# State loaded as it lies and transposed by products with the identity, and a first batch in written order: one core of a Trainium2 chip

## The chip, the cores and the metric

The kernel runs on one core of one Trainium2 chip. The core has a matrix engine (PE in the profile, with its weight loads as PEld), a vector engine (DVE), a scalar engine (ACT), GpSimd (POOL) and SyncE (SP), which here only issues transfers. PE writes to PSUM, eight banks of 2 KB in each of 128 partitions; the other engines copy from there to SBUF, where matmul operands have to lie. The metric is the device time of one launch in microseconds (us); lower is better.

## The reference

Eight batches of an attention between 512 positions `x` and 32 state vectors `state`, in both directions, with 8 heads of 64 numbers; then a feed-forward layer with the activation g = h * tanh(softplus(h)), called Mish, over all 8 x 544 rows.

```python
scores = scale * x @ state.T;   a  = softmax(scores)     # B, H, 512, 32
xread  = a @ state
scores2 = scale * state @ x.T;  a2 = softmax(scores2)    # B, H, 32, 512
sread  = a2 @ x
rows   = concat([xread, sread], axis=2)                  # B, H, 544, 64
x      = rows.transpose(0, 2, 1, 3).reshape(B * 544, 512)
h      = x @ w_in                                        # 512 -> 2048
out    = mish(h) @ w_out                                 # 2048 -> 512
```

The two weights come as 8-byte floats, 8 MB each; the kernel makes 4-byte numbers of them from their two words.

## The kernel before

*Arithmetic.* xread is never formed. Since xread @ w_in = a @ (state @ w_in), the kernel multiplies the state with a slice of w_in (`sw_slice`) and the softmax with that (`gemm1`). The large products run in a 4-byte type that PE takes in one pass, and each operand is split in a high part (a rounded copy) and a low part (the difference), with three products in place of one: high x high, high x low, low x high. So behind most results stand a cast on ACT or DVE (`swh`, `ah`, `gh`, the high half of `wo`) and a subtraction on DVE (`swl`, `al`, `gl`, the low half).

*Slots.* A batch is worked off in eight slots j of 256 hidden columns. In each slot `gemm1` runs 12 matmuls into two PSUM banks `ph`; ACT takes Mish of them into `g`; DVE splits `g` into `gh` and `gl`; `gemm2` runs 24 matmuls (four blocks of tokens, six each) into four banks `acc`, which collect over the eight slots. `second` runs such a `gemm2`, whole or in halves, up to two slots behind its `gemm1` (LAG = 2). The two remaining banks, `misc` (tag "m"), serve everything else in turn: transposes, scores, `sw_slice` and state reads.

*Attention.* `state_blocks` makes `bd`, the transposed state with its heads on two halves of the partitions, so that heads can be multiplied two and four at a time in small tiles of 64 x 32. `x_transposed` (`xt`), `scores`, `soft1_e`, `soft1_n`, `soft1_a` make the softmax over the state, in its two parts `ah` and `al`. The other direction, called the state part here, is `soft2_m` and `soft2_e` (maximum, exp), `e2_transposed` and `sread` (two reads and `sreadT`). Batches 0 and 1 transpose x on PE; from batch 2 on x comes by strided transfers (`xq`, 32 per batch) and DVE transposes it. The attention of the next batch runs in pieces between the slots of this one.

*Batch 0* also makes the weights. Each 512 KB piece of w_in or w_out is loaded as words; ACT scales the high words (`scale_high`) and rounds the low words (`round_low`; POOL may do that), DVE joins them (`join_words`). Slot j + 1 needs piece j + 1 of w_in, and the accumulation of slot j needs piece j of w_out, split in two by `high_w_out` and `low_w_out`. The words, exp and Mish use two different tables of ACT, so a slot of batch 0 loads a table twice.

*Order.* The program is written out in Python; a scheduler with a model of the times then orders the instructions of each engine, by their place in the source and by when it takes them to be ready. `behind(...)` asks that what it encloses be issued after the instructions remembered in `last`; it is used by hand all through batch 0. All loads go through SP's queue in one order, except the state of batch 0, which ACT's queue issues. Buffers order loads too: pieces 4 to 7 of w_in wait for the join of an earlier piece, and piece 7 of w_out for the last use of batch 0's x, which lies in its place (`tag="wo7"`). `fill` issues products of no use to keep PE busy in the head.

The state of a batch is loaded in three transfers of 32 KB, for even heads, odd heads and even heads again, and two transposes make `bd` of it:

```python
sn = pool.tile([P, 3, D], F32, tag="sn", name=f"sn_{b}")
for i in range(3):
    (nc.sync if b else nc.scalar).dma_start(
        sn[:, i, :], state[b].rearrange("(c a) n d -> a c n d", a=2)[i % 2])
...
for s in range(2):
    nc.tensor.transpose(
        pt[:, s * P:(s + 1) * P], sn[:, s:s + 2].rearrange("p a d -> p (a d)"), ident)
```

Of the kernel before, what the change touches and what calls it, by code (L numbers as in the profile page):

```python
# [16 lines left out]
P = 128  # L17
# [10 lines left out]
FILL = 20, 2, 2, 4  # L28
# [9 lines left out]

@with_exitstack
def state_attention_mish_kernel(ctx, tc, x, state, w_in, w_out, out):  # L40

    nc = tc.nc
    nc.scalar.preload_act_table_set("exp_and_others")
# [54 lines left out]
    def scale_high(raw):  # L98

        y = raw[..., 1].bitcast(F32)  # L100
        last["words"] = nc.scalar.activation(y, y, AF.Prelu, scale=2.0 ** -112, alpha=-2.0 ** 32)  # L101

    def round_low(raw, by_pool=False):
        lw = raw[..., 0]
        if by_pool:
            nc.gpsimd.tensor_scalar(lw, lw, 0.876 * 2.0 ** -29, 0.49, ALU.mult, ALU.add)
        else:
            last["words"] = nc.scalar.activation(lw, lw, AF.Copy, scale=0.876 * 2.0 ** -29, bias=0.49)
# [8 lines left out]
    def join_words(raw, to):  # L117
        lw, hw = raw[..., 0], raw[..., 1]
        last["join"] = nc.vector.scalar_tensor_tensor(
            to.bitcast(U32), hw, 3, lw, ALU.logical_shift_left, ALU.bitwise_or)  # L120
# [31 lines left out]
    def high_w_out(j, w):  # L152
        wo[j] = const.tile([P, 2, 2, DM], F32R, tag=f"wo{j}", name=f"wo_{j}")
        last["woh"] = nc.vector.tensor_copy(wo[j][:, :, 1], w)

    def low_w_out(j, w):
        last["wo"] = nc.vector.tensor_sub(wo[j][:, :, 0], w, as_f32(wo[j][:, :, 1]))

    def load_state(b):

        sn = pool.tile([P, 3, D], F32, tag="sn", name=f"sn_{b}")
        for i in range(3):
            (nc.sync if b else nc.scalar).dma_start(
                sn[:, i, :], state[b].rearrange("(c a) n d -> a c n d", a=2)[i % 2])
        return sn

    def state_blocks(b, sn):
# [3 lines left out]
        for s in range(2):  # L171
            nc.tensor.transpose(
                pt[:, s * P:(s + 1) * P], sn[:, s:s + 2].rearrange("p a d -> p (a d)"), ident)
        nc.vector.tensor_copy(bd.rearrange("p s n -> p (s n)"), pt[:, :2 * P])
# [3 lines left out]
    fills = []  # L178
# [10 lines left out]
    xs0 = load_x(0)  # L189
# [3 lines left out]
    for _ in range(WARM):  # L193
        nc.tensor.matmul(warm[:, :P], ident, ident, start=True, stop=True)


    def attention(b, xs, sn, xq=None):
# [4 lines left out]
        def x_transposed(c):  # L202

            if xq is not None:
                xTs[c] = temp(f"xT_{b}_{c}")
                nc.vector.transpose(  # L206
# [4 lines left out]
            for i in range(NT):  # L211
                nc.tensor.transpose(  # L212
                    pt[:, i * P:(i + 1) * P], xs[:, c, i // 2, (i % 2) * P:(i % 2 + 1) * P], ident)
            xTs[c] = temp(f"xT_{b}_{c}")
            if b == 0 and c % 2:
                nc.vector.tensor_copy(xTs[c], pt)
            else:
                nc.scalar.copy(xTs[c], pt)

        def scores():  # L220

            pss = [misc(f"sc_{b}_{u}") for u in range(2)]
            for c in range(NC):
                o = slice(c * NS, (c + 1) * NS)
                for kc in range(2):
                    kp = slice(kc * 2 * P, (kc + 1) * 2 * P)
                    for u in range(2):
                        last["PE"] = nc.tensor.matmul(  # L228
                            pss[u][o, kp], bds[b][half(u), kc ^ u, o], xTs[c][half(u), kp],
# [5 lines left out]
            for u in range(2):  # L235
                o = scs.rearrange("n k (v u p) -> n k v u p", v=2, u=2)[:, :, :, u]
                i = pss[u].rearrange("n (k v p) -> n k v p", k=2, v=2)
                if b == 0 and u:
                    nc.vector.tensor_scalar_mul(o, i, 0.125)
                else:  # L240
                    last[b, "scs"] = nc.scalar.mul(o, i, 0.125)  # L241

        def fill(n, pt):

            for _ in range(n):
                last["PE"] = nc.tensor.matmul(  # L246
# [6 lines left out]
        def soft2_m(kc):  # L253
            nm = nms[kc] = pool.tile([P, 1], F32, tag="nm", name=f"nm_{b}_{kc}")
            nc.vector.tensor_reduce(nm, sc[kc], AX.X, ALU.max, negate=True)

        def soft2_e(kc):
            e2 = temp(f"e2_{b}_{kc}")
            sm = pool.tile([P, 1], F32, tag="sm", name=f"sm_{b}_{kc}")
            last[b, "exp2"] = nc.scalar.activation(e2, sc[kc], AF.Exp, bias=nms[kc], accum_out=sm)  # L260
            nc.vector.tensor_scalar_add(sm, sm, 1e-9)  # L261
            rs2[kc] = pool.tile([P, 1], F32, tag="rs", name=f"rs_{b}_{kc}")
            nc.vector.reciprocal(rs2[kc], sm)
# [6 lines left out]
        def e2_transposed(kc):  # L270
            e2 = e2s[kc]
            pt = misc(f"e2p_{b}_{kc}")
            for t in range(NT):
                nc.tensor.transpose(pt[:, t * P:(t + 1) * P], e2[:, t * P:(t + 1) * P], ident)  # L274
            e2T[kc] = temp(f"e2T_{b}_{kc}", (P, NT, P))
            nc.scalar.copy(e2T[kc].rearrange("p t n -> p (t n)"), pt)
# [14 lines left out]
        def transposed(pt, src):  # L291
            for t in range(NT):
                last["PE"] = nc.tensor.transpose(pt[:, t * P:(t + 1) * P], src[:, t * P:(t + 1) * P], ident)

        def soft1_e():
# [6 lines left out]
            for kc in two:  # L302
                if b == 0:
                    transposed(src[kc], sc[kc])
                else:
                    nc.vector.transpose(e1[kc], sc[kc])  # L306
            for kc in two:
                mx = small["mx"][kc]
                with behind(*(((0, "sub"),) if b == 0 and kc else ())):
                    nc.vector.tensor_reduce(mx, groups(src[kc]), AX.X, ALU.max)  # L310
                last[b, "sub"] = nc.vector.tensor_sub(groups(e1[kc]), groups(src[kc]), wide(mx))
                with behind(*(("words",) if b == 0 else ())):
                    last[b, "exp"] = nc.scalar.activation(e1[kc], e1[kc], AF.Exp)

        def soft1_n():
            for kc in two:
                sm, r1 = small["s1"][kc], small["r1"][kc]
                nc.vector.tensor_reduce(sm, groups(e1[kc]), AX.X, ALU.add)
                nc.vector.tensor_scalar_add(sm, sm, 1e-9)
                nc.vector.reciprocal(r1, sm)  # L320
                last[b, "e1"] = nc.vector.tensor_mul(groups(e1[kc]), groups(e1[kc]), wide(r1))

        def soft1_a():
            for kc in two:
# [3 lines left out]
                else:  # L328
                    at = temp(f"at_{b}_{kc}")
                    nc.vector.transpose(at, e1[kc])  # L330
                hi = pool.tile([P, S], F32R, tag=f"ah{kc}", name=f"ah_{b}_{kc}")
                lo = pool.tile([P, S], F32R, tag=f"al{kc}", name=f"al_{b}_{kc}")
                last[b, "ah"] = nc.scalar.copy(hi, at)
                last[b, "DVE"] = nc.vector.tensor_sub(lo, at, as_f32(hi))
# [7 lines left out]
        def sread(kc):  # L342
            pr = misc(f"srp_{b}_{kc}")
            for t in range(NT):
                for h4 in range(4):
                    o = slice(h4 * NS, (h4 + 1) * NS)
                    last["PE"] = nc.tensor.matmul(  # L347
                        pr[o, :D],
                        e2T[kc][:, t, o],
                        xs[:, h4, kc, t * D:(t + 1) * D],  # L350
# [4 lines left out]
            nc.vector.tensor_scalar_mul(srd[0][:, kc], pr[:, :D], rs2[kc])  # L355

        def sreadT():
            pt = misc(f"srTp_{b}")[:, :P]
            nc.tensor.transpose(pt, srd[0].rearrange("p k d -> p (k d)"), ident)
            ptv = pt.rearrange("p (c n) -> p c n", c=NC)  # L360
            hi, lo = (t[..., b * NS:(b + 1) * NS] for t in srT)
            nc.scalar.copy(hi, ptv)
            nc.vector.tensor_sub(lo, ptv, as_f32(hi))

        xt, s_, s1, s2, e2t, sr = x_transposed, scores, soft1, soft2, e2_transposed, sread
        if b == 0:
# [313 lines left out]
```

## Time and profile before

| | |
|---|---|
| median of 3 runs | 699.71 us (697.62 to 700.04) |
| profiled execution | 697.67 us, its span 695.9 us |
| granted PE clock over the span | 0.992 of full |
| instructions | 10040, of these 4142 matmuls |
| loads and stores | 41.81 MB, 60 GB/s over the span |
| HBM read, written | 32.24 MB, 8.91 MB |

Times in the profile are microseconds from the start of the span. A row of the timeline has the start, the duration, the engine, the source line, the operation, output<-inputs, shape and count, and in brackets the idle time of the engine before it with what ended it. A row of a stretch of time has the busy time and, in parentheses, the instructions of each engine. A row of groups has the count, the total, the mean in ns, and the idle time before. A matmul is shown busy until its modelled end, so that matmuls that follow each other closely overlap.

### The profile page before, as it was taken

Reading aid. Unit: us, or ns where it says so; the run is one execution under the profiler, and the core shown is the slowest. Engines: PE = TensorE matmul, PEld = TensorE weight load, DVE = VectorE, ACT = ScalarE, POOL = GpSimd, SP = SyncE. Lnnn points to the kernel's source line nnn. Section 1 sums busy time; section 2 is a strip of 40 time slices with the busy share of each in tenths; the row PEclk is TensorE's granted clock in tenths of the full one; section 3 lists DMA queues with packets and bytes.
Section 4 is the critical chain, followed back from the end, with each engine's and each line's share of the span. In section 5 each row is a group of like instructions: output and inputs, shape, how many; then the busy total and the mean of one; then the engine's idle time right before and its main releaser. Section 6 shows DMA issues by size and latency. Waiting matters only on the chain.

```text
span 695.9 us, 10040 instructions
## 1 busy us (share of the span) xinstructions
PE 680.2 (98%) x4142; PEld 516.8 (74%) x4142; DVE 344.9 (50%) x520; ACT 262.0 (38%) x415; POOL 12.6 (2%) x13
## 2 busy tenths in 40 slices
PE   6988999999999999999999999999999999999997
PEld 5866776577777777777777777777777788977785
DVE  1996697483349423753367333942384234332221
ACT  2896864261235212641146123531255113222110
POOL 0230000000000000000000000000000000000000
PEclk7999999999999999999999999999999999999999
DMA  9975223401023011311032102301000001000001
GB/s 316 360 248 182 34 34 101 78 10 57 10 73 50 1 61 37 74 18 61 7 86 37 58 4 71 48 6 61 30 31 1 1 1 61 0 9 23 0 1 60
DMA packets 75789, 41.81 MB, mean 60 GB/s; under 512 B 57056, under 2 KB 65248, under 8 KB 75744
## 3 DMA queue, kind: packets, MB, share of 16 engines
q1 hardware_dynamic: 75348, 41.08, 20.3%
q8 instruction: 32, 0.52, 0.3%
q10 hardware_dynamic: 396, 0.10, 0.1%
q14 instruction: 13, 0.11, 0.0%
HBM read 32.24 MB, written 8.91 MB: 59 GB/s over the span
## 4 chain that ended last, share of the span: by engine, by line
PE 93%; ACT 4%; DMA 1%; issue 1%; ACTq 0%; DVE 0%
PE acc L480 51%; PE ph L435 24%; PE swp L398 5%; PE ph_s L458 3%; PE acc_s L480 3%; PE sc L228 2%; PE srp L347 1%; DMA sn<-in_state_dram 1%; PE e2p L274 1%; PE acc L246 1%; ACT L409 1%; ACT wor L101 1%; ACT g L409 1%; PE xTp L212 0%; ACT L101 0%
## 5 line engine op out<-in xcount | busy, mean ns | idle before, releaser
L480 PE MATMUL acc<-wo,gh 128*128 128x512 f32 x1024 | 326.5, 400 | 0.0
L480 PEld LDWEIGHTS acc<-wo,gh 128*128 128x128 f32 x1024 | 188.5, 188 | 67.9 <-issue 22.5
L480 PE MATMUL acc<-wo,gl 128*128 128x512 f32 x512 | 201.2, 396 | 0.0
L409 ACT ACTIVATE g<-ph 128x512 f32<-128x512 f32 x128 | 74.2, 598 | 223.0 <-DVE gl L416 154.7
L414 DVE CAST gh<-g 128x1024 fp32r<-128x1024 f32 x64 | 44.2, 691 | 163.5 <-PE acc L480 146.2
L480 PEld LDWEIGHTS acc<-wo,gl 128*128 128x128 f32 x512 | 96.3, 188 | 23.2 <-DVE gl L416 0.8
L435 PE MATMUL ph<-ah,swh 128*128 128x512 f32 x256 | 84.2, 401 | 2.8 <-ACT swh L403 2.8
L416 DVE TENSOR_TENSOR gl<-g,gh 128x1024 fp32r<-128x1024 f32 x64 | 78.8, 1231 | 4.8
L435 PE MATMUL ph<-al,swh 128*128 128x512 f32 x256 | 79.9, 392 | 0.0
L435 PE MATMUL ph<-ah,swl 128*128 128x512 f32 x256 | 79.3, 393 | 0.0
L404 DVE TENSOR_TENSOR swl<-swp,swh 128x512 fp32r<-128x512 f32 (+1 forms) x72 | 42.8, 625 | 54.2 <-ACT swh L403 53.8
L435 PEld LDWEIGHTS ph<-ah,swh 128*128 128x128 f32 x256 | 47.4, 188 | 17.9 <-ACT swh L403 4.6
L435 PEld LDWEIGHTS ph<-al,swh 128*128 128x128 f32 x256 | 48.2, 188 | 10.2
L435 PEld LDWEIGHTS ph<-ah,swl 128*128 128x128 f32 x256 | 47.6, 188 | 10.6
L403 ACT CAST swh<-swp 128x512 fp32r<-128x512 f32 (+1 forms) x72 | 35.7, 547 | 22.5 <-PE swp L398 22.5
L398 PE MATMUL swp<-w_in_sb,bd 64*32 64x512 f32 (+1 forms) x576 | 41.6, 554 | 1.9 <-DVE sm L261 1.8
L409 ACT ACT_TABLE_LOAD x20 | 25.7, 1283 | 30.1 <-PE e2p L274 14.1
L489 ACT COPY o<-acc 128x512 f32<-128x512 f32 x16 | 9.4, 587 | 43.6 <-PE acc L480 27.4
L455 DVE TENSOR_TENSOR wl<-w_in_sb,wh 128x512 fp32r<-128x512 f32 x16 | 11.1, 692 | 29.1 <-PE ph_s L458 25.1
L206 DVE STREAM_TRANSPOSE xT<-xq 128x512 f32<-128x512 f32 x24 | 24.4, 1091 | 0.1
L487 DVE COPY o<-acc 128x512 f32<-128x512 f32 x16 | 11.0, 689 | 20.5 <-DMA out_dram<-o 14.5
L306 DVE STREAM_TRANSPOSE e<-scs 128x512 f32<-128x512 f32 x14 | 9.1, 691 | 24.1 <-ACT scs L241 24.1
(82 smaller groups left out, 529.5 us busy)
## 6 DMA issues: line engine op xcount, KB each, us to landing
x<-in_x_dram SPq DMA_DIRECT2D x32, 256.0 KB
wir<-in_moe_w_in_dram SPq DMA_DIRECT2D x16, 512.0 KB
wor<-in_moe_w_out_dram SPq DMA_DIRECT2D x16, 512.0 KB
out_dram<-o SPq DMA_DIRECT2D x32, 256.0 KB
xq<-in_x_dram SPq DMA_DIRECT2D x192, 32.0 KB
sn<-in_state_dram SPq DMA_DIRECT2D x21, 32.0 KB
out_dram<-o_s SPq DMA_DIRECT2D x8, 64.0 KB
sn<-in_state_dram ACTq DMA_DIRECT2D x3, 32.0 KB
```

The source lines that it names most:

```text
L206: nc.vector.transpose(xTs[c].rearrange("p (k v i g) -> p g k v i", k=2, v=2, g=4), xq[:, c].rearrange("p k (g v) d -> p g k v d", v=2))
L228: last["PE"] = nc.tensor.matmul(pss[u][o, kp], bds[b][half(u), kc ^ u, o], xTs[c][half(u), kp], start=True, stop=True)
L398: last["PE"] = nc.tensor.matmul(pw[kc][o, :], bds[b][half(kc), 0, o], w_in_sb[half(kc), c, f], start=True, stop=True)
L403: last["swh"] = nc.scalar.copy(hi[:, kc], pw[kc])
L404: last["swl"] = nc.vector.tensor_sub(lo[:, kc], pw[kc], as_f32(hi[:, kc]))
L409: last["mish"] = nc.scalar.activation(g[:, k * 512:(k + 1) * 512], ph, AF.Mish)
L414: nc.vector.tensor_copy(gh, g)
L416: last["gl"] = nc.vector.tensor_sub(gl, g, as_f32(gh))
L435: last["PE"] = nc.tensor.matmul(ph, l, r, start=(i == 0), stop=(i == len(seq) - 1))
L455: nc.vector.tensor_sub(lo, w, as_f32(hi))
L458: nc.tensor.matmul(ph[r][:, k * 256:(k + 1) * 256], l[:, c], srT[i][:, c], start=(c == 0 and n == 0), stop=(c == NC - 1 and n == 2))
L480: last["PE"] = nc.tensor.matmul(accs[key][t], g[:, sl], wo[fc // 2][:, fc % 2, w, :], start=(fc == 0 and n == 0), stop=(fc == NFC - 1 and ...
```

## The change

- `load_state` makes two transfers in place of three, each of four whole heads as they lie in memory. `state_blocks` multiplies each with the identity, twice, for the upper and the lower half of the partitions: four products in place of two transposes. The copy to `bd` orders the heads by a stride, and `scores` and `sw_slice` index it accordingly.
- A class `InOrder` wraps PE, DVE and ACT. While its switch is on, in batch 0, each instruction of an engine is issued after the one written before it. Batch 0 is written out as a sequence of its own, with one accumulation of lag; `behind` is left for loads.
- In batch 0 the parts of the next attention have fixed places: its state block and two x transposes end slot 4, the other two stand in slot 5 with the scores, `soft1_e` stands in slot 6, `soft1_n` and `soft1_a` in slot 7. Its state part (`soft2_m` to `sreadT`) goes to batch 1.
- POOL rounds low words of w_out only from slot 3 on; ACT does those of pieces 1 and 2. w_out's piece 7 is scaled in slot 6 and joined in slot 7.
- `soft1_n` interleaves its two halves in the order written; `gemm1` in slots 0 and 1 goes through both banks in turn; the last `fill` has 6 products in place of 4.
- The loads of `xq` and state for batch 2 stand behind all of batch 0, and x of batch 2 in slot 3 of batch 1.

```diff
-FILL = 20, 2, 2, 4
+FILL = 20, 2, 2, 6
...
+class InOrder:
+    on = False
+    def __init__(self, tc, engine):
+        self.tc, self.engine, self.last = tc, engine, None
+    def __getattr__(self, name):
+        method = getattr(self.engine, name)
+        def issue(*args, **kwargs):
+            with ExitStack() as st:
+                if InOrder.on and self.last is not None:
+                    st.enter_context(self.tc.issue_after(self.last))
+                made = method(*args, **kwargs)
+            self.last = getattr(made, "ins", made)
+            return made
+        return issue
...
+    pe, dve, act = (InOrder(tc, e) for e in (nc.tensor, nc.vector, nc.scalar))
...
-        sn = pool.tile([P, 3, D], F32, tag="sn", name=f"sn_{b}")
-        for i in range(3):
+        sn = pool.tile([P, 2, D], F32, tag="sn", name=f"sn_{b}")
+        for g in range(2):
             (nc.sync if b else nc.scalar).dma_start(
-                sn[:, i, :], state[b].rearrange("(c a) n d -> a c n d", a=2)[i % 2])
+                sn[:, g, :], state[b, 4 * g:4 * g + 4].rearrange("h n d -> (h n) d"))
...
-        for s in range(2):
-            nc.tensor.transpose(
-                pt[:, s * P:(s + 1) * P], sn[:, s:s + 2].rearrange("p a d -> p (a d)"), ident)
-        nc.vector.tensor_copy(bd.rearrange("p s n -> p (s n)"), pt[:, :2 * P])
+        for g in range(2):
+            for r in range(2):
+                pe.matmul(pt[half(r), g * P:(g + 1) * P], sn[:, g], ident, start=True, stop=True)
+        dve.tensor_copy(
+            bd.rearrange("p s (c n) -> p c s n", n=NS),
+            pt[:, :2 * P].rearrange("p (c s n) -> p c s n", s=2, n=NS))
...
+            for step, kc in ((total, 0), (guard, 0), (total, 1), (turn, 0), (guard, 1), (norm, 0), (turn, 1), (norm, 1)):
+                step(kc)
...
+        steps = [(k, i) for k in range(2) for i in range(6)]
+        if b == 0 and j < 2:
+            steps.sort(key=lambda s: s[1] // 2)
...
+    def product(b, j):
+        phs = gemm1(b, j, aTs[b], sw)
+        def finish():
+            g = mish(b, j, phs)
+            gh, gl = high_g(f"{b}_{j}", g)
+            pending.append((b, (2 * j, 2 * j + 1), (gh, gl), NT))
+            return lambda: low_g(g, gh, gl)
+        return finish
...
+    InOrder.on = True
...
+    finish = product(0, 1)
+    at1, _, read = attention(1, sn1)
+    for j in range(1, SLOTS):
+        if j < 7:
+            words(j + 1, j, j > 2)
+        if j == 6:
+            words(None, 7, True)
+        if j + 1 < SLOTS:
+            join_i(j + 1)
+        if j == 3:
+            for kc in range(2):
+                at0["m2"](kc)
+            for kc in range(2):
+                at0["e2"](kc)
+        if j == 4:
+            for kc in range(2):
+                at0["e2t"](kc)
+        if j == 5:
+            at0["srT"]()
+            at1["xt"](2)
+            at1["xt"](3)
+        if j == 6:
+            at1["s1e"]()
+        if j < 7:
+            join_o(j)
+        second((0, 1), True)
+        low = finish()
+        if j + 1 < SLOTS:
+            sw.update(sw_slice(0, j + 1, 1))
+        else:
+            sw.update(sw_slice(1, 0))
+        second((2, 3))
+        if j == 4:
+            for kc in range(2):
+                at0["sr"](kc)
+        if j == 7:
+            at1["s1n"]()
+            at1["s1a"]()
+            join_o(j)
+        low_o(j)
+        low()
+        if j == 4:
+            state_blocks(1, sn1)
+            at1["xt"](0)
+            at1["xt"](1)
+        if j == 5:
+            at1["s"]()
+        if j + 1 < SLOTS:
+            finish = product(0, j + 1)
+    InOrder.on = False
...
+    todo = [lambda: [at1[p](kc) for p in ("m2", "e2") for kc in range(2)]] + read
+    xqs = {2: new_xq(2)}
+    with behind("load"):
+        load_xq(2, xqs[2], range(4 * H))
+        sn_next = load_state(2)
...
+        if key == 1 and j < 2:
+            second((2 * j, 2 * j + 1), j == 0)
+        elif len(pending) > LAG:
             second()
```

More of the change, by code (lines that the diff above doesn't have):

```diff
@@ L387, in attention @@
         ]
-        return [], pieces, aT
+        return own, ahead, read
     def sw_slice(b, j, n=2):
@@ L511, in state_attention_mish_kernel, with second, words @@
     with behind("load"):
-        xs_next, sn_next = load_x(1), load_state(1)
+        xss[1], sn1 = load_x(1), load_state(1)
     load(("o", 4), ("o", 6), ("o", 5), ("i", 6), ("i", 7), ("o", 7))
-    first[0]()
-    with behind((0, "scs")):
-        scale_words(raws[0])
-    first[1]()
+    pending = []
+    def second(ts=None, keep=False):
+        k_, fcs, g_, nt = pending[0] if keep else pending.pop(0)
+        gemm2(k_, list(fcs), g_[0], g_[1], nt, ts)
+    def words(i=None, o=None, by_pool=False):
+        for raw, p in ((raws.get(i), False), (rawo.get(o), by_pool)):
+            if raw is not None:
+                round_low(raw, True) if p else None
+                scale_high(raw)
+                None if p else round_low(raw)
@@ L519, in state_attention_mish_kernel, with fill @@
+    def fill(i):
+        at0["fill"](FILL[i], accs[0][NT - 1])
+    sw, aTs = {}, {}
+    InOrder.on = True
+    at0, _, _ = attention(0, sn0)
+    aTs[0] = at0["aT"]
+    at0["xt"](0)
+    at0["xt"](1)
+    state_blocks(0, sn0)
+    at0["xt"](2)
+    at0["xt"](3)
+    at0["s"]()
+    words(0)
+    at0["s1e"]()
     new_accs(0, NT)
-    def fill(i):
-        with behind("PE"):
-            fills[0](FILL[i], accs[0][NT - 1])
     fill(0)
-    first[2]()
-    with behind((0, "exp")):
-        scale_words(raws[1])
@@ L529, in state_attention_mish_kernel @@
-    with behind((0, "e1")):
-        join_w_in(0, raws.pop(0))
-    with behind("PE", "words", "join"):
-        first[3]()
+    words(1)
+    at0["s1n"]()
+    join_i(0)
+    at0["s1a"]()
     fill(1)
-    with behind("PE", (0, "ah"), (0, "DVE")):
-        sw_next = sw_slice(0, 0, 1)
+    sw.update(sw_slice(0, 0, 1))
     fill(2)
-    ws = {}
-    with behind("swl"):
-        join_w_in(1, raws.pop(1))
-    with behind("swh", "join"):
-        scale_words(rawo[0])
-        ws[0] = join_w_out(0, rawo.pop(0))
@@ L638, in state_attention_mish_kernel @@
-        for _ in range((0, 0, 1, 1)[j] if key == 0 and j < 4 else 1 + (key == 0)):
+        if key + 1 < B and j == 0:
+            own, ahead, rd = attention(key + 1, sn_next, xqs.pop(key + 1))
+            aTs[key + 1] = own["aT"]
+            todo = todo + ahead + rd
+        g = split_g(f"{key}_{j}", mish(key, j, gemm1(key, j, aTs[key], sw)))
+        pending.append((key, (2 * j, 2 * j + 1), g, NT))
+        nb, nj = (key, j + 1) if j + 1 < SLOTS else (key + 1, 0)
+        if nb < B and nj % 2 == 0:
+            sw.update(sw_slice(nb, nj))
```

275 lines of the change are left out of this document (106 added, 169 removed).

## The prediction

> **What bounds the kernel now.** I read the page's busy shares first, then the view by stretches of time, because a share of 98% is a mean over stages with different limits.
>
> ```profile
> span 695.9 us, 10040 instructions
> ...
> PE 680.2 (98%) x4142; PEld 516.8 (74%) x4142; DVE 344.9 (50%) x520; ACT 262.0 (38%) x415; POOL 12.6 (2%) x13
> ```
> ```profile
> 25.80:118.80 93.00, 87.35 (x633) 64.64 (x632) 74.68 (x107) 70.45 (x97) 10.77 (x6) 1.00 0.45 141
> 118.80:140.00 21.20, 21.20 (x128) 12.62 (x126) 11.02 (x17) 5.68 (x11) 0.00 (x0) 1.00 0.44 94
> ```
>
> The columns are PE, PEld, DVE, ACT and POOL busy, then clock and DMA. Up to 118.8 us, where the second batch's first product ends, PE is idle for 93.00 - 87.35 = 5.65 us, and DVE and ACT are busy for three quarters of the time. After that PE has no idle time, so any matmul added there costs its full length and DVE, ACT and DMA are hidden. The change can win only in the first 119 us, and can lose anywhere. PE also wastes time while busy. Small products of 64x32 run side by side, so half a set takes as long as a whole one:
>
> ```profile
> 122.00:123.40 1.40, 1.06 (x8) 0.15 (x8) 1.00 1.03 310
> 125.00:126.40 1.40, 1.06 (x8) 0.15 (x8) 1.00 0.32 49
> ...
> 135.20:136.40 1.20, 1.04 (x2) 0.14 (x2) 1.00 0.35 54
> 139.10:140.40 1.30, 1.08 (x14) 0.17 (x14) 1.00 0.32 49
> 157.80:159.10 1.30, 1.09 (x16) 0.18 (x16) 1.00 0.00 0
> ```
> ```profile
> 129.00:130.40 1.40, 1.09 (x16) 0.47 (x16) 1.00 0.36 57
> 132.50:133.90 1.40, 1.09 (x16) 0.47 (x16) 1.00 0.30 47
> 204.90:206.50 1.60, 1.13 (x32) 0.61 (x32) 1.00 0.30 47
> ```
>
> These are the state-times-w_in product (first fence) and the scores (second). Batch 1 splits three sets, 1.0 us lost each. So what the change can touch, beside the head, is 5.65 + 3.0 = 8.65 us.
>
> The head shows in PE's timeline and in its clock (third number from the right in the stretches):
>
> ```profile
> 7.28 0.30 PE L172 MATMUL st<-ident,sn 128*128 128x128 f32 x1 [1.07 <-DMA sn<-in_state_dram]
> 9.88 0.47 PE L172 MATMUL st<-ident,sn 128*128 128x128 f32 x1 [2.29 <-DMA sn<-in_state_dram]
> 10.15 1.91 PE L212 MATMUL xTp<-ident,x 128*128 128x128 f32 x8
> 11.99 2.81 PE L228 MATMUL sc<-xT,bd 64*32 64x256 f32 x32
> 15.56 1.97 PE L293 MATMUL scT<-ident,scs 128*128 128x128 f32 x8 [0.76 <-ACT scs L241]
> ```
> ```profile
> 5.90:9.00 3.10, 0.61 (x4) 1.00 1.00 338
> 9.00:10.00 1.00, 0.12 (x1) 0.64 0.99 384
> 10.00:15.00 5.00, 4.80 (x41) 0.50 1.04 404
> 15.00:19.00 4.00, 3.44 (x16) 0.50 1.05 398
> ```
>
> The first state transpose needs two of the three loads and starts at 7.28; the second needs the third and starts at 9.88. In the stretch to 9 PE is busy for 0.61 of 3.10 us, and then the clock is at half until 19. Scores take 2.81 us there, 1.13 at full clock.
>
> **The change part by part.** The sum is made against the profiled execution's own 697.67 us, 2.0 below the median of 699.71.
>
> *State as it lies.* Two loads instead of three, so both have landed at 7.28, where the first transpose started. A 128-column matmul takes about 0.107 us at full clock (eight in 1.91 at half is at most 0.24 each). The eight halves of the four products, two side by side, take 0.43: 7.28 to 7.7. This is the last copy before the scores:
>
> ```profile
> 12.10 0.69 DVE L216 COPY xT<-xTp 128x512 f32<-128x512 f32 x1 [1.28 <-PE xTp L212]
> ```
>
> The block copy, priced like it, frees a PSUM buffer at about 8.4; the last four x transposes end at 8.85, and the copy of them at 9.8, instead of 12.8. Scores then end 3.0 us earlier if the clock falls as now. If it stays full, 0.9 of the scores' remaining half and 0.4 of the softmax's first transpose go too: 4.3. I take the middle, **-3.6**; nothing in the trace says on which side the busier stretch falls. From there to the first real product the order on DVE and ACT is the one that the trace shows, so all shifts alike; its loads of weights stay ahead.
>
> Weighed here: the Trainium skill, "TensorE: Matmul & The Clock Gate", section "HAM oscillation — how this bites in real kernels", says the clock falls after an idle gap longer than about 3.4 us. This trace disagrees in size: gaps of 1.07 and 2.29 us, with 0.3 of work between, were enough. By the page the shorter new gap would keep full clock, and the head's term would be -4.3.
>
> *The same products in batches 1 to 7.* Two transposes (0.22) become 0.43 of products and about 0.1 for entering and leaving the small tile form: 0.3 each, on a full PE: 7 x 0.3 = **+2.1**. Bounds: 1.4 (no such switch), 5.2 (nothing side by side: 0.86 + 0.1 - 0.22 = 0.74). I take the value near the low end, since the rows above show halves running side by side. One load less per batch on SP hides under the full PE; the copy with its new stride too.
>
> *Source order in batch 0.* PE, DVE and ACT each keep the written order. Prices:
>
> ```profile
> 54.78 1.09 ACT L409 ACTIVATE g<-ph 128x512 f32<-128x512 f32 x2
> 55.75 0.66 ACT L403 CAST swh<-swp 128x256 fp32r<-128x256 f32 x2
> 56.42 1.28 ACT L101 ACT_TABLE_LOAD   x1
> 57.72 1.16 ACT L101 ACTIVATE wir<-wir 128x1024 f32<-128x1024 f32 x1
> 58.76 1.13 ACT L108 ACTIVATE wir<-wir 128x1024 uint32<-128x1024 uint32 x1
> 59.78 1.21 ACT L101 ACTIVATE wor<-wor 128x1024 f32<-128x1024 f32 x1
> ```
> ```profile
> L119 DVE SCALAR_TENSOR_TENSOR w<-wor 128x1024 uint32<-128x1024 uint32 x2 | 2.5, 1252 | 0.0
> L416 DVE TENSOR_TENSOR gl<-g,gh 128x1024 fp32r<-128x1024 f32 x2 | 2.4, 1200 | 0.0
> ...
> L330 DVE STREAM_TRANSPOSE at<-e 128x512 f32<-128x512 f32 x2 | 1.3, 685 | 0.0
> L311 DVE TENSOR_TENSOR e<-e,mx 128x512 f32<-128x512 f32 x2 | 1.3, 690 | 0.0
> ```
> ```profile
> 155.27 2.74 PE ph L435 x12
> 158.01 1.02 PE swp L398 x16
> 159.03 5.79 PE acc L480 x24
> ```
>
> A slot needs 2.74 + 5.79 + about 0.65 (half-width state product) = 9.2 of PE. ACT in slots 1 and 2, with w_out's low words moved to it from POOL, needs two table loads, four word passes, Mish and the casts: 2.56 + 4.65 + 1.09 + 0.66 = 9.0. Covered by 0.2, so slots 1 to 3 run without the idle time that they have now. If DVE slows beside POOL, that cover is gone and the excess shows at once. Four more fill instructions hide in PE's wait for the casts. Then:
>
> Slot 4: the state block and two x transposes of batch 1 share two PSUM buffers; the third waits for an ACT copy: 0.9 (2.1 if buffers go by turns, since the block copy is queued behind two low passes on DVE).
>
> Slot 5: the last x transpose waits for copies that stand behind words(6, 5) on ACT: 1.28 + 3.5 + 0.3 = 5.1, against PE's 2.74 + 0.4 of cover: 2.0.
>
> Slot 6: from the end of batch 1's scores: two copies 1.3 (priced like Mish, with 0.2 of handing over), table 1.28, two word passes 2.3, then on DVE join 1.25, two transposes, two maxima, two subtractions (6 x 0.69 = 4.1), exp 0.55 priced like Mish, table 1.28, Mish 1.09, first cast 0.33: 13.5. PE has 2.74 + 5.79 + 0.65 = 9.2: **4.3 idle** before product 7.
>
> Slot 7: after the state product of batch 1: casts and a difference 1.9 (like Mish and one pass of 0.69), then sums and norms 4 x 0.69, and per half a transpose 0.69, ACT cast 0.55, difference 0.69: 1.9 + 2.8 + 3.9 = 8.6. PE has half the accumulation, 2.9: 5.7, less two early matmuls: **5.5 idle** before product (1, 0). Queued behind these on DVE are w_out 7's join and slot 7's low part, so its accumulation isn't there to fill with.
>
> Sum 12.7, less 0.16 at each of four gaps (a matmul is shown busy for 0.40 and spaced 0.24): 12.1.
>
> *State part of attention 1 in batch 1.* It is free of the fixed order, so it can fall into those gaps:
>
> ```profile
> L347 PE MATMUL srp<-x,e2T 128*32 128x64 f32 x64 | 1.1, 221 | 0.0
> L274 PE MATMUL e2p<-ident,e 128*128 128x128 f32 x8 | 1.0, 273 | 0.0
> ```
>
> That is 2.1 of work, leaving 10.0. Bounds: nothing (12.1), everything that batch 2 could lend as well (2.3, for the two long gaps' 9.8 filled). Batch 1's split sets: between 0 and 3.0, I take 1.0. So 11.0 against 8.65: **+2.35**. The loads for batch 2 that move on SP go behind the weights, where no PE wait is shown.
>
> Sum: 697.67 - 3.6 + 2.1 + 2.35 = **698.5**.
>
> **The rivals.** *A, the forecast*: waits move from slots 2 and 5 to slots 6 and 7 and eat what the state load gives.
>
> *B, faster*: batch 1's free instructions fill the long gaps. For: 9.8 us of gap, and DVE and ACT have holes of their own there. Against: scores of batch 2 need 32 strided loads and four DVE transposes first. Half of the 7.7 left filled gives 694.6; all, 690.8. It decides from 2.3 us more than I count.
>
> *C, slower*: the clock falls in the gaps of slots 6 and 7. For: the head fell with 0.61 of 3.10 us busy, and a 4.3 or 5.5 us gap leaves no more in one such stretch. Price if it lasts 9 us as there: 4.5 each, 703.0 for one and 707.5 for both; I take 705. It decides from 4.7 us lost. Against: filled as in A, the gaps are in pieces. The Trainium skill's same page, Part 1, lets the full clock return after one busy window of 3.4 us: 1.7 each, 701.9 for both. The head doesn't show that return so early.
>
> *D, the load brings nothing*: the second load lands at 9.88, as the third does: 698.5 + 3.6 + 0.2 = 702.3. For: the same queue beside the same x. Against: the first two do land by 7.28.
>
> **How the numbers follow.** About 0.5%, 3.5 us, can be told from no change, so "same" is 696.2 to 703.2. A 0.38, B 0.36, C 0.17, D 0.09. Faster is B, 0.36; slower is C with a little of A, 0.18; the rest, 0.46, the same. A's own range is 696.2 to 702, with products at 1.4 to 5.2 and slots 4 and 5 as bounded. For 8 in 10 I go from B with all filled, 691, to C's middle, 704.5.
>
> **What would show it.** Right: the state products start near 7.3 us and product (0, 0), now at 25.8, near 22.2; no PE wait in slots 1 to 3; PE waiting for a cast of slot 7's state product after about 90 us, and for the cast or difference of batch 1's weights some 15 us later. Wrong: a state load landing after 9 us; a clock of 0.5 after 85 us; transposes or state reads of attention 1 filling the long gaps; eight state products that take 0.8 us or more in batches 2 to 7, which would put 3 us on the whole.

## The result: 706.83 us against 699.69, slower by 1.0%

| | before | after |
|---|---|---|
| median of 6 runs each | 699.69 us (697.62 to 700.22) | 706.83 us (703.54 to 707.9) |
| profiled execution, its span | 697.67, 695.9 us | 703.54, 701.8 us |
| granted PE clock over that span | 0.992 | 0.997 |

The ratio of after to before is 1.010, with a 95% interval of 1.0076 to 1.0124. The forecast was 698.5 in a range of 691 to 704.5; the time lies above it. The profiled executions differ by 5.87 us, the medians by 7.14. Medians here and below leave out three executions of other kernels, at 745.0, 747.66 and 1729.16 us, which stand far outside the rest of their runs.

The page of the changed kernel, its first lines:

```profile
span 701.8 us, 10128 instructions
...
PE 681.9 (97%) x4194; PEld 516.0 (74%) x4194; DVE 346.9 (49%) x520; ACT 264.6 (38%) x417; POOL 8.0 (1%) x11
```

The span grew by 5.9 us and PE's busy time by 1.7 only, so most of the loss is idle time. The view by stretches of the changed kernel says where; it has the same two stretches as in the prediction, with PE, PEld, DVE, ACT and POOL busy, then the clock:

```profile
25.80:118.80 93.00, 80.73 (x536) 57.60 (x536) 69.42 (x97) 64.07 (x88) 7.28 (x5) 0.98 0.38 121
118.80:140.00 21.20, 21.20 (x168) 15.90 (x166) 10.60 (x16) 6.28 (x12) 0.00 (x0) 1.00 0.28 72
```

In the same 93 us PE does 6.6 us less than before (80.73 against 87.35). DVE and ACT do less too (69.42 and 64.07 against 74.68 and 70.45): no engine is fuller than it was. (The changed kernel's slots begin 5.3 us earlier, so its stretch holds somewhat other work; the waits are the firmer measure.) The view of waits, for PE in that stretch, names what ended each wait, with the total, the number and the longest in us. First the changed kernel, then the one before:

```profile
PE ph L53 <- ACT swh L53: 3.5, 1, 3.5
PE ph L53 <- ACT ah L53: 3.5, 1, 3.5
PE xTp L53 <- DVE srT_l L53: 2.8, 1, 2.8
PE e2p L53 <- ACT e L53: 1.4, 1, 1.4
PE xTp L53 <- ACT xT L53: 0.7, 1, 0.7
PE swp L53 <- DVE w_in_sb L53: 0.3, 1, 0.3
```
```profile
PE ph L435 <- ACT swh L403: 2.8, 3, 1.8
PE swp L398 <- DVE sm L261: 1.8, 1, 1.8
PE xTp L212 <- ACT xT L218: 1.0, 1, 1.0
```

12.2 us of waits against 5.6. (Line 53 is the wrapper that issues every instruction of the changed kernel, so its rows are told apart by output and inputs.) The longest come late in batch 0: the wait for srT_l stands in slot 5, the one for swh before product 7, the one for ah before product (1, 0).

The head did better than forecast. The timeline of PE, changed kernel, then the row before's first product of slot 0:

```profile
6.35 1.12 PE L53 MATMUL st<-ident,sn 128*64 128x128 f32 x8
...
8.78 1.80 PE L53 MATMUL sc<-xT,bd 64*32 64x256 f32 x32
...
20.51 0.78 PE L53 MATMUL ph<-ah,swh 128*128 128x512 f32 x2
```
```profile
25.82 0.96 PE L435 MATMUL ph<-ah,swh 128*128 128x512 f32 x3
```

All eight state products start at 6.35 with no wait for a transfer, and product (0, 0) starts 5.3 us earlier. After batch 1 the same transposition costs in every batch. The next instruction starts 0.59 us after the eight products, 0.14 after the two transposes, and the pair of matmuls ahead of them takes 0.55 us in place of 0.45:

```profile
265.64 0.61 PE L53 MATMUL ph<-ah,swl 128*128 128x512 f32 x2
266.19 0.66 PE L53 MATMUL st<-ident,sn 128*64 128x128 f32 x8
266.78 0.72 PE L53 MATMUL acc<-wo,gh 128*128 128x512 f32 x2
```
```profile
262.14 0.62 PE L435 MATMUL ph<-ah,swl 128*128 128x512 f32 x2
262.59 0.38 PE L172 MATMUL st<-ident,sn 128*128 128x128 f32 x2
262.73 0.70 PE L480 MATMUL acc<-wo,gh 128*128 128x512 f32 x2
```

The first scores of batches 3 to 7 start at 208.68, 284.83, 361.00, 437.15 and 513.31, so a batch takes 76.16 us; before they started at 205.17, 280.77, 356.38, 431.99 and 507.61, 75.61 apart.

Last, the clock. The stretches of PE around the wait before product (1, 0), changed kernel (busy, clock):

```profile
105.70:109.10 3.40, 0.73 (x2) 1.00 0.00 0
109.90:113.40 3.50, 3.14 (x12) 0.51 0.00 0
113.40:116.80 3.40, 3.40 (x24) 1.00 0.02 5
```

PE works 0.73 of 3.40 us, then runs at half clock for about 3.4 us, then at full clock again.

### The profile page after: what moved, and what is told of

The parts are those of the page before. It is cut to its first block, busy times and chain, and to the rows that moved or that the text cites. A ratio compares the mean times of both kernels' runs of the same rounds, so it can differ in the third digit from the quotient of the medians.

```text
span 701.8 us, 10128 instructions
## 1 busy us (share of the span) xinstructions
PE 681.9 (97%) x4194; PEld 516.0 (74%) x4194; DVE 346.9 (49%) x520; ACT 264.6 (38%) x417; POOL 8.0 (1%) x11
## 4 chain that ended last, share of the span: by engine, by line
PE 94%; ACT 2%; DVE 2%; issue 0%; DMA 0%; POOL 0%; ACTq 0%; POOLq 0%; DVEq 0%
PE acc L53 51%; PE ph L53 25%; PE swp L53 5%; PE ph_s L53 3%; PE acc_s L53 3%; PE sc L53 1%; PE srp L53 1%; PE e2p L53 1%; DVE e L53 1%; PE st L53 1%; ACT L53 1%; ACT wir L53 1%; PE xTp L53 1%; PE warm L53 0%; DVE s L53 0%
## 5 line engine op out<-in xcount | busy, mean ns | idle before, releaser
L53 PE MATMUL swp<-w_in_sb,bd 64*32 64x512 f32 (+1 forms) x576 | 39.9, 554 | 0.4 <-DVE w_in_sb L53 0.3
L53 PE MATMUL acc_s<-wo,gh_s 128*128 128x512 f32 x64 | 20.3, 395 | 0.0
```

Source lines behind the costliest of these rows:

```text
L53: made = method(*args, **kwargs)
```

## The experiments

The theory at the outset: the strict order, with batch 1's softmax at fixed places in slots 6 and 7, makes the waits; the state products cost seven times some 0.5 us; the head's gain is real and smaller than the two together. Rivals: the falls of the clock make the loss; the products make it; the fixed order itself makes it, whatever its sequence.

**State part alone.** The kernel before with the edits of `load_state`, `state_blocks` and the two index changes, nothing else.

> The kernel before with the state part of the change alone (two loads as they lie, four products, the strided copy, the new indices); order, waits and lag as before. Theory: the head gives 5.3 us (product (0, 0) starts at 20.5 instead of 25.8, as in the changed kernel's trace) and the products take 0.55 us per batch from batch 1 on (the batch period grew from 75.61 to 76.16), 3.9 in seven batches: 1.4 us less in all, 698.3 for the median. Rival 1, the head's gain is an effect of the fixed order: product (0, 0) stays near 25.8 and the time is 703. Rival 2, the batch period grew because of the other moves: period 75.6 and the time 694.4.

Measured: 699.15 us against 699.52, ratio 0.999 (0.9958 to 1.0023). In its trace product (0, 0) starts at 20.42 and a batch takes 76.16 us. So the state part wins 5.4 us in the head of the profiled execution and pays 0.55 us in each of seven batches, 3.9 in all. What should be left, 1.5 us, is smaller than the interval: by itself the state part is worth nothing that these runs can tell. Both rivals are out, by the product's start and by the batch period.

**State part undone.** The changed kernel with three loads and two transposes per batch, as before.

> The changed kernel with the state part undone (three loads, two transposes, old indices), all the rest as changed. Theory, the waits of the fixed order cost the same with or without the state part: head at 25.8, batch period 75.6, so 706.8 + 5.3 - 3.9 = 708.2, and PE waits for the cast before product 7 of batch 0 (about 4 us) and before product (1, 0) (about 6 us). Rival, the waits come from the products standing in the shared PSUM buffers: the waits shrink and the time falls below 704.

Measured: 706.26 us, ratio 1.0102 (1.0043 to 1.0162). A batch takes 75.61 us again, and the waits are those of the changed kernel. The view of waits of this kernel, same stretch:

```profile
PE ph L53 <- ACT swh L53: 3.6, 1, 3.6
PE ph L53 <- ACT ah L53: 3.5, 1, 3.5
...
```

So the waits do not come from the state part, and the state part is hardly worth anything here too. The time is 2 us below the 708.2 expected, because the head was not that of the kernel before: product (0, 0) starts at 22.61, not 25.8. The second state transpose starts at 8.40 in place of 9.88, and half clock lasts 3.4 us there (8.35 to 11.76), where the kernel before had 10.2. Against this execution the new load's head is worth 2.1 us (22.61 to 20.51), against the profiled one of before 5.3: what the head is worth depends on how long half clock lasts in the execution that it is compared with.

**Slot 7 in another order.**

```diff
+        if j == 7:
+            at1["s1n"]()
+            at1["s1a"]()
         second((0, 1), True)
         low = finish()
...
         if j == 7:
-            at1["s1n"]()
-            at1["s1a"]()
             join_o(j)
```

> The changed kernel with sums, norms, transposes and casts of batch 1's softmax weights moved from the end of slot 7 to its beginning, ahead of the accumulation and of Mish; nothing else. Theory, the wait before product (1, 0) stands in DVE's written order behind the state product: the wait of about 6 us goes, and with it the stretch at half clock that follows it (3.4 us of it in the profiled run, 1.7 lost): 699 to 701. Rival, DVE and ACT are short of time in slots 6 and 7 whatever the order: the wait moves to product 7 or to the accumulation of slot 7 and the time stays at 705 to 707.

Measured: 700.95 us, ratio 1.0034 (1.0006 to 1.0061), 5.9 us less than the changed kernel's median. Its waits:

```profile
PE ph L53 <- ACT swh L53: 5.4, 2, 3.5
PE xTp L53 <- DVE srT_l L53: 2.3, 1, 2.3
...
```

The wait for ah is gone, 1.9 us of waiting for swh has come in its place, and e2p waits no more: with the 0.7 and 0.3 for xT and w_in_sb, which are unchanged, 8.7 us in all, 3.5 fewer. So normalising and splitting batch 1's softmax at the end of slot 7 was a costly place. The other 2.4 us of the 5.9 are not in the waits of this trace. At the equal clock of 0.993 seven of these runs took 700.19 to 702.73 us and two of the changed kernel 705.8 and 706.35, 4.6 us between the means; the rest I leave unassigned. The half clock that was to go with the wait did not go: this trace has it from 92.6 to 99.4 and from 109.64 to 113.05.

**Slots 5, 6 and 7 in another order.** As above, and `soft1_e` at the end of slot 6 and slot 5's transposes at its start.

```diff
+        if j == 5:
+            at0["srT"]()
+            at1["xt"](2)
+            at1["xt"](3)
         if j < 7:
             words(j + 1, j, j > 2)
...
-        if j == 6:
-            at1["s1e"]()
...
+        if j == 6:
+            at1["s1e"]()
         if j == 4:
             state_blocks(1, sn1)
```

(The first hunk moves the three calls of slot 5 ahead of that slot's words; they stood behind the joins. Slot 7 has the edit shown before.)

> The changed kernel with all three long waits of batch 0 treated: slot 7 as in the run before, batch 1's first softmax part moved to the end of slot 6 (behind Mish, casts and low parts), and in slot 5 the state transpose and the two x transposes with their copies ahead of the words. Theory, each wait stands in the written order and in nothing else: from 700.95 the 3.9 before product 7 and 2.5 of slot 5 go, and with them most of the falls of the clock: 694 to 696. Rival, DVE and ACT have no room left in slots 5 to 7, so a wait taken from one place comes back in the next: 699 to 701.

Measured: 705.5 us, ratio 1.0074 (1.0052 to 1.0095). Worse than with slot 7 alone, and above both expectations. Its waits and two rows of PE's timeline behind them:

```profile
PE ph L53 <- ACT swh L53: 7.2, 2, 6.5
PE swp L53 <- DVE w_in_sb L53: 2.9, 2, 2.6
...
PE xTp L53 <- DVE srT_l L53: 0.2, 1, 0.2
```
```profile
77.23 0.67 PE L53 MATMUL swp<-w_in_sb,bd 64*32 64x256 f32 x16 [2.64 <-DVE w_in_sb L53]
...
109.57 1.65 PE L53 MATMUL ph<-ah,swh 128*128 128x512 f32 x3 [6.53 <-ACT swh L53]
```

Slot 5's wait for srT_l fell from 2.3 to 0.2 and came back 6 us later as a wait of 2.6 for the join of w_in; slot 6's wait of 3.5 is gone and came back in slot 7, whole. The rival had this right, though not the time. I read it so, that the same ACT and DVE work stood in one line either way and moving a step only chose which product waits for it. One wait of 6.5 us is also worse than two of 3.5: this kernel's clock by stretches (busy, clock) shows

```profile
105.40:115.60 10.20, 6.03 (x16) 0.50 0.00 0
```

half clock for 10.2 us, where the changed kernel had 3.4.

**The same with batches 1 to 7's state as before.** Batch 0 keeps the new load and the products, by `if b < 1`.

> The same with the state of batches 1 to 7 loaded and transposed as in the kernel before (three loads, two transposes), and only that of batch 0 as it lies. Theory, the products cost 0.55 us in each batch of a full PE and their gain is in the head alone: 3.5 to 3.9 us less than the kernel that it is run beside with products in all batches. Rival, the longer batch period comes from their place between other small tiles and not from their number: less than 1.5.

Measured: 701.4 us, ratio 1.0006 (0.9982 to 1.003), 4.1 us less than the kernel that it was run beside, and a batch takes 75.61 us again. That is the price of the products in seven batches.

**Order switched off.** The changed kernel with `InOrder.on = False`.

> The changed kernel with the switch for the written order left off, all else as changed: the scheduler orders batch 0 by the new sequence's priorities, with no hand-written waits. Theory, the fixed order makes the waits (an instruction that is ready stands behind one that is not): PE's waits before products 7 and (1, 0) shrink below 2 us each and the time is 699 to 703. Rival, the new sequence with its shorter lag makes them, fixed or not: 705 to 708.

Measured: 715.35 us, ratio 1.0206 (1.016 to 1.0251). Neither time held. The loss is in the head. PE's timeline of this kernel, and one of its stretches (busy, clock):

```profile
23.85 1.68 PE L53 MATMUL swp<-w_in_sb,bd 64*32 64x256 f32 x16 [4.75 <-DVE e L53]
30.28 1.41 PE L53 MATMUL swp<-w_in_sb,bd 64*32 64x256 f32 x16 [4.75 <-DVE swl L53]
...
35.31 2.08 PE L53 MATMUL ph<-ah,swh 128*128 128x512 f32 x4
```
```profile
22.40:39.50 17.10, 9.04 (x63) 0.50 1.05 388
```

Product (0, 0) starts 14.8 us later than with the order on, since the scheduler, left free, puts later work ahead of batch 0's softmax. Behind that, the theory's waits did shrink: before product 7 PE waits 2.0 us in place of 3.5, and before product (1, 0) not at all. The view of waits from 35.3 to 140 us, its longest row:

```profile
PE ph L53 <- ACT swh L53: 2.0, 1, 2.0
```

From product (0, 0) to the end of the span this kernel takes 678.7 us, the changed one 681.3. This does not settle whether the fixed order makes the waits, since ACT and DVE had 14.8 us more for the weights before the slots began. On the whole the new source is worse without its order than with it.

**Products of no use in the two long waits, first try.** 16 and 22 products of the identity with itself before product 7 and product (1, 0), into these products' own banks.

> The changed kernel with products of no use put into the two long PE waits: 16 into the bank of product (0, 7) and 22 into that of product (1, 0), each before the product starts and overwrites the bank. They take no work away, so only the clock can change. Theory, of the 706.83 some 3 to 4 us are the half clock that follows the waits (runs with a granted clock of 0.990 took 707.3 to 707.5, the one with 0.997 took 703.5): 702.5 to 704, clock 0.997 or more in every run. Rival, the clock falls in the head and not in the waits: clock and time as in the changed kernel, 706 to 707.

Measured: 707.69 us, ratio 1.0126 (1.0081 to 1.0171), at clocks of 0.995 to 0.999. Inconclusive: product 7's bank is free only once Mish has read it, so its fills started at 93.94, at the end of the wait, and put product 7 at 97.53 in place of 94.63; product (1, 0) starts at 112.04 in place of 108.13. The fills kept the clock up and cost about what that gained.

**Products of zeros in the three long waits.** A tile of zeros times the identity, added to an open accumulator, which needs no bank.

```diff
+    def keep(n):
+        for _ in range(n):
+            pe.matmul(accs[0][NT - 1][:, :P], zero, ident, start=False, stop=False)
...
         if j == 5:
             at0["srT"]()
+            keep(14)
             at1["xt"](2)
...
+        if j > 5:
+            keep(18 if j == 6 else 18)
         if j + 1 < SLOTS:
             finish = product(0, j + 1)
```

> The changed kernel whole; in the three long waits of the first batch (before the third and fourth set of x transposes of batch 1, before product 7, before product (1,0)) TensorE multiplies a tile of zeros with the identity and adds it to an open accumulator: 14, 18 and 18 products of 128 columns, which need no bank of their own and so can start when the wait starts. They add zero to the result. By the 0.17 us of one such product in the fills of the head they take 2.4, 3.1 and 3.1 us of waits of 3.1, 3.9 and 3.9. Theory (the falls of the clock in the waits make the difference between the profiled 703.5 and the median 706.8): the clock stays at 0.997 or above in the runs and the median comes to 701 to 703.5. Rival (the falls cost little; the waits alone make the loss): 706 to 708, whatever the clock. Should the products not lie in the waits, they add up to 8.5 us: 712 and above.

Measured: 703.86 us, ratio 1.009 (1.0058 to 1.0123), just above the theory's range. PE's timeline and its stretches, this kernel:

```profile
91.09 4.18 PE L53 MATMUL acc<-ident,zero 128*128 128x128 f32 x36
95.03 0.71 PE L53 MATMUL ph<-ah,swh 128*128 128x512 f32 x2
...
104.70 4.18 PE L53 MATMUL acc<-ident,zero 128*128 128x128 f32 x36
108.64 0.71 PE L53 MATMUL ph<-ah,swh 128*128 128x512 f32 x2
110.48 1.36 PE L53 MATMUL e2p<-ident,e 128*128 128x128 f32 x8 [1.14 <-ACT e L53]
```
```profile
105.70:109.10 3.40, 3.40 (x31) 1.00 0.00 0
109.90:113.40 3.50, 2.87 (x20) 1.00 0.00 0
```

The fills (18 of them, shown as 36 passes) lie in the waits: product 7 starts at 95.03 in place of 94.63, product (1, 0) at 108.64 in place of 108.13. One such product takes 0.22 us here (18 in 3.94), not the 0.17 of the expectation, so they outlast the waits a little. The clock is 0.998 to 1.000 in these runs. The median is 3.0 us lower than that of the changed kernel: about so much the falls cost. It is still 4.2 us above the kernel before, which has half clock of its own, in the head (9.3 to 19.5 us in its profiled execution). At equal clock the difference is larger: runs of before at 0.997 took 694.78 to 695.86 us here, the changed kernel's one run at 0.997 took 703.54. The clock is a cost of both kernels, in other places, and not what tells them apart.

**Parts put together.** Three kernels: the changed one with slot 7's edit and the state of batches 1 to 7 as before; the same with products of zeros (12, 18 and 10) in its waits; and the kernel before with the new load and products in batch 0 alone:

```diff
+        if b < 1:
+            sn = pool.tile([P, 2, D], F32, tag="sn", name=f"sn_{b}")
+            for g in range(2):
+                (nc.sync if b else nc.scalar).dma_start(
+                    sn[:, g, :], state[b, 4 * g:4 * g + 4].rearrange("h n d -> (h n) d"))
+            return sn
         sn = pool.tile([P, 3, D], F32, tag="sn", name=f"sn_{b}")
```

This last one was run twice, each time beside the kernel before.

> The kernel before with batch 0's state loaded as it lies and multiplied with the identity, all other batches as before. Theory: the head's 5.4 us stay and the 0.55 per batch go: 694 to 696, batch period 75.6. Rival, the head's gain is given back at the waits in slots 2 and 5, which stand on other things (the join of w_in's third piece, a cast) and where the clock may fall: 698 to 700, since the state part alone came out at 699.15 against 699.52.

> The kernel before, with only batch 0's state loaded as it lies and transposed by products; the same kernel as in the earlier run, whose profile was of no use. Theory: 695.1 again (694 to 696.5); in the trace the first product of slot 0 starts at 20.4 to 20.6 us instead of 25.8, and the scores of the later batches follow each other after 75.6 us, not 76.16. Rival (the earlier gain was chance of the clock): 698 to 700.

> The changed kernel with two edits: the normalisation and the split of batch 1's attention moved from the end of slot 7 to its start, and the state of batches 1 to 7 loaded twofold and transposed as before (batch 0 as it lies, with products). Theory (the terms add up): 700.95 of the first edit alone less 3.9 to 4.1 for the products of seven batches (seven times 0.55 us of batch period) = 697, bounds 695.5 to 698.5. Rival (the products' cost is hidden here): 700 to 702.

> The kernel with the two edits (slot 7's attention steps at its start, state of batches 1 to 7 as before), and 12, 18 and 10 products of zeros in the three waits that are left. They add zero to the result. Theory (the clock's falls cost some us where the waits let it fall): 694 to 696, with a clock of 0.997 and above. Rival (they cost nothing): the same as without the products of zeros, 696.5 to 698.5. If the products delay the work behind them: up to 7 us more.

| | median, us | ratio to before |
|---|---|---|
| before, batch 0's state new (first time) | 694.18 | 0.9929 (0.9901 to 0.9956) |
| the same, second time | 695.05 | 0.9953 (0.9927 to 0.998) |
| slot 7 and old state in batches 1 to 7 | 698.35 | 1.0001 (0.998 to 1.0022) |
| the same with products of zeros | 696.72 | 0.9985 (0.9957 to 1.0013) |

The first kernel beats both the one before and the changed one, as forecast. PE's timeline of its second time:

```profile
20.45 0.72 PE L449 MATMUL ph<-ah,swh 128*128 128x512 f32 x2
```

The head is that of the changed kernel, and a batch takes 75.61 us as before. The rival's falls of the clock came too: in this trace two stretches of 3.5 us behind the waits of slots 2 and 5, from 41.8 and 65.7, ran at a clock of 0.53, but they did not take the gain back. At a clock of 0.999 the kernel took 692.37 to 692.82, and the kernel with the products in all batches 695.83 and 695.92: 3.3 us for seven batches, near the 4.1 above. Of the other two, slot 7's edit and the old state come to 698.35 where 697 was forecast, inside its bounds; the products of zeros come to 696.72, above the theory's 694 to 696, and gain 1.6 us, inside the noise of the two intervals.

## Why the prediction was wrong

By its own terms, profiled execution against profiled execution:

| term | forecast | measured | from |
|---|---|---|---|
| head | -3.6 | -5.3 | product (0, 0) at 20.51, was 25.82 |
| state products, batches 1 to 7 | +2.1 | +3.7 | five batches of 0.55 longer, two of 0.45 (0.59 less 0.14) |
| waits of batch 0 | 10.0 against 5.65 | 12.2 against 5.6 | the views of waits |
| split sets | 1.0 against 3.0 | 2.5 against 3.0 | the rows below |
| two more fills ahead of product (0, 1) | 0 | 0 | from product (0, 0) to (0, 1) 5.03 us, was 5.01 |
| clock | 0 (rival C: 4.5 a fall) | +1.1 | e2p to the next set: 3.40 us, 2.34 where the clock held |
| sum | +0.85 | +5.6 | the profiled executions differ by 5.87; 0.3 is not assigned |

**The step that failed is the one behind the waits: "That is 2.1 of work, leaving 10.0".** The waits themselves came where the working put them and at nearly its sizes: slot 4 0.7 (0.9 forecast), slot 5 2.8 (2.0), slot 6 0.3 and 3.5 (4.3), slot 7 3.5 and 1.4 (5.5); 12.2 in all against 12.1 by the forecast before anything was taken off, and none in slots 1 to 3. But the 2.1 did not come off them. Of attention 1's state part only the eight transposes e2p came forward, into the gap behind slot 7, and they had to wait there for their own exp (1.4 us "<- ACT e"): ACT and DVE, whose lateness makes the gap, are the engines that have to feed what was to fill it. The state reads came at 122.6, when the gap was over. The exps even stood in the way. DVE had the second half of batch 1's weights ready for its cast `ah` at 109.42; ACT did two exps first and cast it from 110.82 on, and the rest of product (1, 0) starts at 111.88. The timelines of DVE and of ACT, changed kernel:

```profile
108.72 0.70 DVE L53 STREAM_TRANSPOSE at<-e 128x512 f32<-128x512 f32 x1
```
```profile
109.39 0.72 ACT L53 ACTIVATE e<-scs,nm 128x512 f32<-128x512 f32 x1
...
110.82 0.60 ACT L53 CAST ah<-at 128x512 fp32r<-128x512 f32 x1
```

So e2p filled part of a gap that its own exps had made some 1.4 us longer; this is read from the trace, and no run took the exps out. The gain that the rival B expected from the holes of DVE and ACT did not come either. In these runs work filled a wait only if it didn't hang on the engine that is waited for: the products of zeros, which hang on none, did.

**The split sets were the second.** I took 1.0 us; the timeline of PE shows two sets of sw_slice in halves, each half as long as a whole (the second set's at 181.57 and 186.22), and a split set of state products:

```profile
100.55 1.09 PE L53 MATMUL swp<-w_in_sb,bd 64*32 64x512 f32 x16
...
113.66 1.06 PE L53 MATMUL swp<-w_in_sb,bd 64*32 64x512 f32 x8
...
116.25 1.06 PE L53 MATMUL swp<-w_in_sb,bd 64*32 64x512 f32 x8
...
188.81 0.43 PE L53 MATMUL st<-ident,sn 128*64 128x128 f32 x2
189.60 0.65 PE L53 MATMUL st<-ident,sn 128*64 128x128 f32 x6
```

Twice 0.97 (two halves of 1.0 to the next start, against 1.02 for a whole set), 0.35 for the state products (0.36 and 0.58, against 0.59), and some 0.2 for a split state read: 2.5.

**The products were mis-sized.** 0.43 and 0.1 of switching had been put down for the eight, and 0.59 was measured; but the two transposes had been put at 0.22 and take 0.14 to the next start. That is 0.45; the last 0.1 of the 0.55 by which a batch grew stands ahead of the set, where the pair of matmuls takes 0.55 in place of 0.45. The sum stayed inside the bounds (1.4 to 5.2). The warning sign given in the prediction, 0.8 us or more a set, did not appear, and the 3 us on the whole came nevertheless, because it was tied to the set's own length and not to the difference.

**The head was right in kind and too small.** The forecast let the first product start at 7.28, where the first transpose had started; the loads of whole heads were there by 6.35. That is 0.9, and the rest is the clock: it stayed full, the case that the bound of 4.3 was worked out for. The two together are 5.2, and 5.3 was measured. The size is luck in part: the execution compared with had 10.2 us of half clock in its head, and against the run with the old state, which had 3.4, the term is 2.1. Rival D is out.

**Rival C came, small, beside A.** The clock fell in slot 7 as its condition said, after 0.73 of 3.40 us busy. It cost 1.1 us in the profiled execution, not 4.5, since it lasted one stretch of 3.4 us and not 9. That the measured time lies near this rival's 705 is chance. The prediction had weighed the Trainium skill, "TensorE: Matmul & The Clock Gate", Part 1, section "What's actually happening", by which the full clock returns after one busy window of 3.4 us, against the 9 us of the head, and sided with the head. In the changed kernel the page's value is the right one. Nor does the head speak against it: in its three stretches of 3.4 us at half clock, from 9.28 on, PE is busy for 2.81, 2.66 and 3.41 us, and the full clock is back after the third, the first that is busy throughout. In the kernel with slots 5 to 7 in another order it was the same (0.00, 2.61 and 3.41 us from 105.35 on). But with the state part alone half clock lasted 6.8 us from 65.4 on with PE shown as busy throughout, so what ends it is not settled here. Over the runs the falls cost the changed kernel 3.0 us in the median, but hardly separate it from the kernel before, which loses about as much (4.6 us between its median of 699.7 and its runs at 0.997).

From the profiled executions to the medians another 1.3 us are added: the profiled run of the changed kernel was its fastest, 3.3 below its median, that of before 2.0 below.

**What the experiments settle.** Shown is that the waits come with the new batch 0 and not with the state part (they stay when that is undone), that slot 7's place for the softmax alone is worth 5.9 us by the medians and 4.6 at equal clock, that the products cost 3.3 to 4.1 us, and that the clock is not the difference (4.2 us are left when it is held). Not shown is which trait of the new batch 0 makes the other waits: the fixed order as such, the places of the steps, or the lag of one accumulation, which no run changed by itself. That every wait in slots 5 to 7 comes from one chain on ACT and DVE is argued from the way they moved; no run took work off that chain.

## What to carry to other kernels

A gain that falls due once and a cost that falls due in every batch have to be multiplied out before they are put in together: the new state load was worth 4.6 us (699.7 to 695.05) when it was used in batch 0 alone, and nothing that the runs can tell when it was used in all eight. Where a wait is to be covered, list what the cover waits for: work that needs the late engine comes late itself, and moving a step of the late engine's line moves the wait. Compare two kernels at equal clock before a clock is blamed.

## What the runs showed of the hardware that I had not expected

One and the same kernel spends a different time at half clock from run to run. The kernel before took 694.78 to 695.86 us at a mean clock of 0.997 and 700.06 to 702.48 at 0.987. The Trainium skill, "TensorE: Matmul & The Clock Gate", Part 1, section "What's actually happening", says that the gate's window runs freely, and that the same kernel therefore has a different number of slow matmuls from run to run. The runs agree with that, in that a wait of the same length brought half clock in some executions and not in others: the wait before product 7, 3.5 us, left the clock full in the changed kernel's profile, and in that of the same kernel with the old state it fell there. The stretches of PE of the latter, the wait before product 7 first (busy, clock):

```profile
93.60:97.00 3.40, 0.91 (x4) 1.00 0.32 50
97.10:100.50 3.40, 3.40 (x10) 0.50 0.13 19
110.80:117.50 6.70, 5.56 (x18) 0.50 0.00 0
```

Half clock came in lengths near multiples of 3.4 us: 3.4 here and in the changed kernel, 6.7 after the second wait here, 10.2 after the wait of 6.5 us in the kernel with slots 5 to 7 in another order, and 17.1 in the head of the kernel with the order switched off.
